# A spectral layer and a dense layer, twice: first rows straight from x, scales on the small matrix, turns row by row, W2 in pieces, the filter rebuilt

## Chip, cores and metric

One core of a Trainium2 chip. The time is device time in microseconds of one execution of the whole kernel; the runs of the kernel before took 1265.25 us (median of 3 runs, 1263.46 to 1265.83).

## What is computed

`x` is 2048 x 1024 in bf16. Two different residual layers, A and B, run one after the other, and then both once more with the same weights:

```python
def A(x, w_r, w_i):              # spectral layer
    X = rfft2(x.astype(float32)) * (w_r + 1j * w_i)
    return irfft2(X, s=(2048, 1024)).astype(bfloat16)

def B(x, w1, b1, w2):            # dense layer, F = 3584
    h = x @ w1 + b1
    sp = log1p(exp(-abs(h))) + where(h > 0, h, 0)
    return (h * tanh(sp)) @ w2   # Mish

x = x + A(layernorm(x)); x = x + B(layernorm(x))
x = x + A(layernorm(x)); x = x + B(layernorm(x))
```

The layernorm takes the mean of each row away, so column 0 of the transform is zero; the kernel uses columns 1 to 512 of the filter alone.

## The kernel before

Everything runs on one core, with x resident in SBUF as `XS` (16 tiles of 128 rows). Work is written in program order for each engine; a helper records each operation with the buffers that it reads and writes and puts semaphore waits in front of it, so that each engine's queue (PE, DVE, ACT, POOL, SP) runs strictly in the order written. All DMAs are issued through one helper line, L242.

**Layer A** splits the transform. A row index n is 128 n2 + n1, a column is 128 h + l. `XR` holds the normalised x with the 128 pairs (n2, h) on the partitions. To get there each normalised tile is written to `xn_scratch` in memory and read back in another shape (`xn_store`, `xr_load`, L460 to L470), both on POOL's queue. Stage S1 (`s1`, L486) multiplies `XR` for each n1 by the 128 x 128 matrix `M` (the transforms over n2 and over h in one) into `Y`. Then 8 groups of two k2 slots go through a pipeline of 12 steps: s2 (the rest of the transform over columns, tables FD), s3 (over n1, tables FT, and the product with the filter on DVE), i1 and i2 (back, tables BT and BD). In each step, group g is in s2, g-1 in s3, g-3 in i1 and g-4 in i2. i2 leaves `U` of its group, 128 l on the partitions and 16 components; `u_turn` (L708) writes it to `u_scratch` in memory and reads it back into `UT` with the components on the partitions, both on SP's queue. The tables of the next groups are loaded behind it on the same queue.

The filter needs reversed rows: in the first layer A `filter_bins` (L546) loads raw rows of w_r and w_i (`WR`), lets 12 matmuls for each group reverse them, copies the parts together into `WT` (POOL and ACT), and also stores `WT` in `w_scratch`. The second layer A loads `WT` from there.

**Layer B** begins with the last stage of the transform, `i4` (L759): 128 columns of `UT` against `MT`, added to `XS` by DVE (L770), rows of the first 8 tiles first. Then the statistics (DVE L412, ACT L393), `scales` (an inverse square root by iteration on DVE, L429 to L443), `apply` (L455, ACT L453), and `transposed` (L798). The first dense matmul `mm1` (L816, Mish on ACT L820) goes over 4 chunks c of 512 rows, two at a time, in 14 rounds fg; the second half of `i4` is spread over the first 8 rounds. W1 comes in 14 pieces for each pair of chunks, each reloaded as soon as the last reader of its buffer is through. W2 is loaded in round 8, in four DMAs, since its place overlaps `UT` and `Y`. `mm2` (L833, added by DVE L838) goes tile by tile; in the first layer B it also makes the statistics, scales and the normalised tile for the next layer A, stored and reloaded as above; loads of the first 12 tiles are written behind chunk 2, because `XR` overlaps the activations of that chunk.

Of the kernel before, what the change touches and what calls it, by code (L numbers as in the profile page):

```python
# [7 lines left out]
P = 128  # L8
# [111 lines left out]
def make_tables():  # L120
    n2, dh = np.arange(16.0), np.arange(8.0)
    reps = [None] * P
    for g in range(8):
# [3 lines left out]
        for kd, c in ((0, 0), (4, 1)):  # L127
            own += [(a, 3, c), (b, 3, c)] + [(s, kd, cc) for (s, cc) in low]
# [7 lines left out]
    cD = np.concatenate([8 * (np.arange(64.0) + 1), 4 + 8 * np.arange(64.0)])  # L136
# [13 lines left out]
    gain[63] = 0.5  # L150
# [14 lines left out]
    return dict(M=M.transpose(1, 0, 2).reshape(P, P), MT=M.reshape(P, P).T, JT=np.concatenate([J, -J, J0, -J0], axis=1),  # L165
# [9 lines left out]
class KB:  # L175
# [120 lines left out]
    def build(self):  # L296
# [3 lines left out]
        self.con = {k: v.ap().bitcast(BF) for k, v in con.items()}  # L300
        self.xn_d = nc.dram_tensor("xn_scratch", (16, P, self.D), BF, kind="Internal").ap()
        self.u_d = nc.dram_tensor("u_scratch", (8, P, 16, P), BF, kind="Internal").ap()
        self.w_d = nc.dram_tensor("w_scratch", (16, P, 2, 512), BF, kind="Internal").ap()
        from contextlib import ExitStack
        with ExitStack() as es:
            def sb(name, shape, dtype=BF):
                return es.enter_context(nc.sbuf_tensor(name, [P] + shape, dtype))
            self.XS = sb("XS", [16, self.D])
# [9 lines left out]
            self.RS = sb("RS", [4, 16], F32)  # L318
            self.PS = es.enter_context(nc.psum_tensor("PS", [P, 8, 512], F32))
# [40 lines left out]
    def prologue(self):  # L360
        sp, dve = self.sp, self.dve
        for j in range(16):
            self.dma(sp, self.XS[:, j, :], self.x[0, j * P:(j + 1) * P, :], f"x{j}", writes=[self.r_xs[j]])
        self.dma(sp, self.M[:], self.con["M"], "m", writes=[self.r_m])
        jt = self.alloc("JT", self.o["JT"], [4 * P])
        self.JT, self.r_jt = jt.ap, jt.res
        self.dma(sp, jt.ap, self.con["JT"], "jt", writes=[jt.res])
        self.dma(sp, self.FD[:], self.con["FD"], "fd", writes=[self.r_fd])
        self.junk = self.alloc("JUNK", self.o["JUNK"], [self.D])
        self.w1_next = 0  # L370

    def constants(self):

        sp, dve = self.sp, self.dve
        self.dma(sp, self.BD[:], self.con["BD"], "bd", writes=[self.r_bd])
# [4 lines left out]
        self.op(dve, lambda e: e.tensor_copy(self.B1[:], self.B1h[:]), reads=[r], writes=[self.r_b1])  # L380
# [7 lines left out]
    def stats_act(self, j):  # L388
        act = self.act
        x, sums, rs = self.XS[:, j, :], self.BN[:, j, 0:2], self.r_mv[j]  # L390
        rs.begin()
        for i, f in enumerate((ACT.Copy, ACT.Square)):
            self.op(act, lambda e, i=i, f=f: e.activation(self.junk.ap, x, f, accum_out=sums[:, i:i + 1]),  # L393
                    reads=[self.r_xs[j]], writes=[self.junk.res], parts=[rs])
# [65 lines left out]
    def xn_store(self, j, b):  # L460
        b.unread = False
        self.dma(self.pool, self.xn_d[j], b.ap, "xw" + b.res.name[2:], reads=[b.res], writes=[self.r_xnd[j]])

    def open_xr(self):
        self.XR = self.alloc("XR", self.o["XR"], [P, P])
        self.XR.res.begin()

    def xr_load(self, j):
        self.dma(self.pool, self.XR.ap[j:P:16, :, :], self.xn_d[j].rearrange("n (h l) -> h n l", l=P), f"xr{j % 4}",
                 reads=[self.r_xnd[j]], parts=[self.XR.res])  # L470

# [14 lines left out]
    def s1(self):  # L486
# [480 lines left out]
```

## Time and profile before

| what | us |
|---|---|
| median of 3 runs | 1265.25 |
| profiled execution, its time | 1271.47 |
| its span, first to last instruction | 1269.7 |
| PE busy with matmuls | 976.2 |
| DVE, ACT, POOL busy | 366.8, 315.1, 85.4 |

A busy PE is one that has a matmul in its pipeline. Views show the start of a group of instructions in us, how long it lasts, the engine, the line, and what was written from what; "idle before" is how long the engine stood before it and what ended that. "SPq" and "POOL ... DMA_DIRECT2D" are issues of DMAs, not transfers. Buffers in the common region of SBUF are all shown as ARENA.

### The profile page before, as it was taken

How to read it: one execution, taken by the hardware profiler on the slowest of the kernel's cores; microseconds unless marked ns; L12 is line 12 of the kernel's file. 1: busy time of each engine (PE TensorE's matmuls, PEld its weight loads, DVE VectorE, ACT ScalarE, POOL GpSimd, SP SyncE). 2: the span in 40 equal slices, each digit the busy share in tenths (PEclk: the TensorE clock that was granted, in tenths of full speed). 3: DMA queues.
4: the chain of work that ended last, by engine and by line, in shares of the span. 5: the costliest groups of instructions: out<-in, count | busy, mean ns of one | idle time of the engine just before them, and what ended most of it. 6: DMA issues, size and time to landing. Idle time of an engine off the chain costs nothing.

```text
span 1269.7 us, 13587 instructions
## 1 busy us (share of the span) xinstructions
PE 976.2 (77%) x5737; PEld 509.6 (40%) x5832; DVE 366.8 (29%) x755; ACT 315.1 (25%) x430; POOL 85.4 (7%) x132
## 2 busy tenths in 40 slices
PE   0000698449969999999997387449959999999998
PEld 0000566325424444444443354334424444444444
DVE  3220486172501443000433286282410111000111
ACT  6000466143321001432000265333312000343000
POOL 0222352000000000000031100000000000000000
PEclk9999998679979999999999598779979999999999
DMA  9333257701462001220069227731272000220000
GB/s 289 74 76 79 78 163 189 167 24 51 140 208 67 25 20 39 76 74 1 26 60 121 59 86 192 153 71 45 87 250 84 25 17 26 83 67 17 17 26 25
DMA packets 130988, 107.19 MB, mean 84 GB/s; under 512 B 43504, under 2 KB 109168, under 8 KB 130928
## 3 DMA queue, kind: packets, MB, share of 16 engines
q1 hardware_dynamic: 123760, 89.41, 25.1%
q0 software_dynamic: 7168, 16.91, 7.9%
q8 instruction: 46, 0.75, 0.3%
q14 instruction: 14, 0.11, 0.0%
HBM read 81.01 MB, written 25.17 MB: 84 GB/s over the span
## 4 chain that ended last, share of the span: by engine, by line
PE 63%; DMA 18%; DVE 9%; issue 5%; ACT 3%; POOL 3%; SPq 0%; DVEq 0%; POOLq 0%; ACTq 0%
PE PS L816 30%; PE PS L833 27%; DMA xn_scratch<-ARENA 9%; POOL ARENA L242 3%; DMA ARENA<-in_B_w_dram 2%; DVE XS L770 1%; PE PS L798 1%; DMA ARENA<-c_bt 1%; DMA u_scratch<-ARENA 1%; DVE BN L412 1%; DMA ARENA<-c_ft 1%; ACT ARENA L635 1%; PE PS L657 1%; DMA ARENA<-xn_scratch 1%; PE PS L494 1%
## 5 line engine op out<-in xcount | busy, mean ns | idle before, releaser
L816 PE MATMUL PS<-ARENA 128*128 128x512 bf16 x1750 | 394.9, 384 | 36.7 <-DMA ARENA<-in_B_w_dram 25.7
L833 PE MATMUL PS<-ARENA 128*128 128x512 bf16 x1754 | 387.7, 379 | 2.0
L816 PEld LDWEIGHTS PS<-ARENA 128*128 128x128 bf16 x1792 | 175.5, 99 | 247.6 <-issue 38.4
L820 ACT ACTIVATE ARENA<-PS,B 128x512 bf16<-128x512 f32 x224 | 153.4, 687 | 471.7 <-PE PS L816 471.6
L833 PEld LDWEIGHTS PS<-ARENA 128*128 128x128 bf16 x1792 | 174.7, 98 | 207.6
L838 DVE TENSOR_TENSOR XS<-PS,XS 128x512 bf16<-128x512 f32 x64 | 44.2, 691 | 562.3 <-PE PS L833 562.3
L494 PE MATMUL PS<-M,ARENA 128*128 128x128 bf16 x256 | 20.9, 257 | 166.5 <-DMA ARENA<-xn_scratch 166.3
L494 PEld LDWEIGHTS PS<-M,ARENA 128*128 128x128 bf16 x256 | 19.7, 119 | 167.9 <-issue 166.7
L500 ACT ACTIVATE ARENA<-PS 128x1024 bf16<-128x1024 f32 x16 | 16.1, 1022 | 244.1 <-PE PS L494 243.7
L412 DVE BATCH_NORM_STATS2 BN<-XS 128x6 f32<-128x512 bf16 x104 | 67.1, 674 | 4.8 <-DMA XS<-in_A_x_dram 3.6
L770 DVE TENSOR_TENSOR XS<-PS,XS 128x512 bf16<-128x512 f32 (+1 forms) x48 | 38.9, 861 | 100.3 <-PE PS L765 100.3
L455 DVE TENSOR_SCALAR ARENA<-XS,RS 128x1024 bf16<-128x1024 bf16 x56 | 29.4, 544 | 78.7 <-DMA xn_scratch<-ARENA 77.9
L657 PE MATMUL PS<-ARENA 128*128 128x256 bf16 x256 | 39.4, 306 | 14.2 <-DMA ARENA<-c_bt 14.2
L242 POOL DMA_DIRECT2D xn_scratch<-ARENA x32 | 18.4, 576 | 450.2 <-DVE ARENA L455 450.2
L242 POOL DMA_DIRECT2D ARENA<-xn_scratch x32 | 34.2, 1072 | 139.4 <-DMA xn_scratch<-ARENA 119.8
L765 PE MATMUL PS<-MT,ARENA 128*128 128x64 bf16 x512 | 21.8, 206 | 27.5 <-issue 26.5
L635 ACT ACTIVATE ARENA<-PS 128x1024 bf16<-128x1024 f32 x32 | 32.9, 1027 | 33.6 <-PE PS L631 33.6
L798 PE MATMUL PS<-IDENT,ARENA 128*128 128x128 bf16 x256 | 21.8, 240 | 23.1 <-DVE ARENA L455 22.0
L664 ACT ACTIVATE ARENA<-PS 128x1024 bf16<-128x1024 f32 x32 | 32.8, 1025 | 24.6 <-PE PS L657 24.6
L657 PEld LDWEIGHTS PS<-ARENA 128*128 128x128 bf16 x256 | 27.4, 109 | 26.9 <-issue 15.9
L393 ACT ACTIVATE ARENA<-XS 128x1024 bf16<-128x1024 bf16 x24 | 25.3, 1056 | 49.9 <-DVE XS L770 44.8
L502 DVE CAST ARENA<-PS 128x1024 bf16<-128x1024 f32 x16 | 18.8, 1218 | 59.3 <-PE PS L494 59.2
(52 smaller groups left out, 524.4 us busy)
## 6 DMA issues: line engine op xcount, KB each, us to landing
ARENA<-in_B_w_dram SPq DMA_DIRECT2D x56, 512.0 KB, 3.8
ARENA<-in_B_w_dram SPq DMA_DIRECT2D x8, 1792.0 KB, 16.0
xn_scratch<-ARENA POOLq DMA_DIRECT2D x32, 256.0 KB, 5.4
ARENA<-xn_scratch POOLq DMA_DIRECT2D x32, 256.0 KB, 6.4
u_scratch<-ARENA SPq DMA_DIRECT2D x16, 512.0 KB, 3.3
ARENA<-u_scratch SPq DMA_DIRECT2D x16, 512.0 KB, 5.2
XS<-in_A_x_dram SPq DMA_DIRECT2D x16, 256.0 KB, 6.1
w_scratch<-ARENA SPq DMA_DIRECT2D x16, 256.0 KB, 3.3
```

Of the source, the lines that this page charges most:

```text
L242: return eng.dma_start(out_ap, in_ap).then_inc(ds.sem, 16)
L412: self.op(self.dve, lambda e: e.bn_stats(self.BN[:, j, 6 * h:6 * h + 6], self.XS[:, j, 512 * h:512 * h + 512]), reads=[self.r_xs[j]], part ...
L494: fns.append(lambda e, q=q, j=j, ps=ps: e.matmul(ps[:, q * P:(q + 1) * P], self.XR.ap[:, 8 * j + q, :], M[:], start=True, stop=True))
L635: self.op(act, lambda e: e.activation(x.ap.rearrange("p a b -> p (a b)"), ps, ACT.Copy, scale=SIG), reads=banks, writes=[x.res])
L657: fns.append(lambda e, c=c, part=part: e.matmul(ps[:, c * 256:(c + 1) * 256], yk.ap[:, part, c * P:(c + 1) * P], t[:, (128, 0)[part]:(384, ...
L664: self.op(act, lambda e: e.activation(v.ap[:, :, i, :], src, ACT.Copy), reads=banks, parts=[v.res])
L770: self.op(self.dve, lambda e: e.tensor_tensor(xs, src, xs, ALU.add), reads=rb, parts=self.r_xs[lo:lo + 8])
L798: fns.append(lambda e, db=db: e.transpose(PSb[:, bank, db * P:(db + 1) * P], xn.ap[:, db * P:(db + 1) * P], self.IDENT[:]))
L816: fns.append(lambda e, db=db, bank=bank, fl=fl: e.matmul(PS[:, bank, :], wb.ap[:, db, fl * P:(fl + 1) * P], x.ap[:, db, :], start=(db == 0 ...
L820: self.op(act, lambda e, bank=bank, ft=ft: e.activation(at.ap[:, ft, :], PS[:, bank, :], ACT.Mish, bias=self.B1[:, ft:ft + 1]), reads=[sel ...
L833: fns.append(lambda e, ft=ft: e.matmul(PS[:, bank, :], at.ap[:, ft, t * P:(t + 1) * P], W2[ft // 7].ap[:, ft % 7, h * 512:(h + 1) * 512], ...
L838: self.op(dve, lambda e: e.tensor_tensor(xs, PS[:, bank, :], xs, ALU.add), reads=[self.r_bank[bank]], writes=[self.r_xs[j]])
```

## The change

- First layer A: `XR` is loaded straight from x in 32 DMAs on SP, and x itself in 4 DMAs. The scale of each row goes on the matrix instead: `first_scales` computes all 16 tiles' scales, turns them with a spread and one fp32 transpose so that each partition (n2, h) has its scale for each n1, and makes 128 scaled copies of the matrix (`MN`) on DVE and ACT. The means are not taken away; they fall on column 0 alone.
- `u_turn` writes each component (row of `UT`) directly from `U` by a DMA of its own, 8 after each half of i2, from SP, POOL and, for the last group, ACT.
- Tables and filter rows are loaded from POOL's queue, `xn_store` moves to SP's. The filter is rebuilt in the second layer A too; `w_scratch` and `u_scratch` go. Copies in `filter_bins` are merged by two.
- `i4` does the first 4 tiles, then the next 4 through ACT into a buffer that DVE adds later; the second half starts in round 2, four at a time.
- W2 comes in 28 pieces, two in each round, and mm2 sums in that order.
- The last tile of the first layer B goes to `XR` by 8 DMAs from SBUF, without memory. Some table layouts, buffer places and the engine of a few copies change.

```diff
     def prologue(self):
+        for c in range(4):
+            self.dma(sp, self.XS[:, 4 * c:4 * c + 4, :], xt[:, 4 * c:4 * c + 4, :], f"x{c}", writes=self.r_xs[4 * c:4 * c + 4])
...
+        xv = self.x[0].rearrange("(n2 n1) (h l) -> h n2 n1 l", n2=16, l=P)
+        for q in range(4):
+            r = Res(f"xr{q}")
+            for h in range(8):
+                self.dma(sp, self.XR.ap[h:P:8, 32 * q:32 * q + 32, :], xv[h][:, 32 * q:32 * q + 32, :], f"xr{q}", parts=[r])
+            self.r_xr.append(r)
+        self.dma(sp, self.FD[:], self.con["FD"], "fd", writes=[self.r_fd])
-        for j in range(16):
-            self.dma(sp, self.XS[:, j, :], self.x[0, j * P:(j + 1) * P, :], f"x{j}", writes=[self.r_xs[j]])
     def constants(self):
-        self.op(dve, lambda e: e.tensor_copy(self.B1[:], self.B1h[:]), reads=[r], writes=[self.r_b1])
+        self.op(self.pool, lambda e: e.tensor_copy(self.B1[:], self.B1h[:]), reads=[r], writes=[self.r_b1])
     def xn_store(self, j, b):
-        self.dma(self.pool, self.xn_d[j], b.ap, "xw" + b.res.name[2:], reads=[b.res], writes=[self.r_xnd[j]])
+        self.dma(self.sp, self.xn_d[j], b.ap, "xw" + b.res.name[2:], reads=[b.res], writes=[self.r_xnd[j]])
+    def xr_direct(self, j, b):
+        for h in range(8):
+            prog = self.act if h % 2 else self.sp
+            self.dma(prog, self.XR.ap[16 * h + j:16 * h + j + 1, :, :], b.ap[:, h * P:(h + 1) * P], "xd" + prog.name,
+                     reads=[b.res], parts=[self.XR.res])
+    def first_scales(self):
+        for j in range(0, 16, 4):
+            for i in range(2):
+                self.stats_dve(j + i)
+                self.stats_act(j + 2 + i)
+            self.sums_to_mv(j + 2, 2)
+        self.scales(0, 16)
...
+        for j in range(16):
+            for q in range(8):
+                n = 8 * j + q
+                if q % 3 == 2:
+                    self.op(act, lambda e, n=n: e.activation(self.MN.ap[:, n, :], self.M0.ap, ACT.Copy, scale=rc[:, n:n + 1]),
+                            reads=[rt.res, self.M0.res], parts=[self.r_mn[j]])
+                else:
+                    self.op(dve, lambda e, n=n: e.tensor_scalar(self.MN.ap[:, n, :], self.M0.ap, rc[:, n:n + 1], None, op0=ALU.mult),
+                            reads=[rt.res, self.M0.res], parts=[self.r_mn[j]])
     def s1(self, li):
-            self.group(fns, reads=[self.XR.res, self.r_m], writes=banks)
+                m = M[:] if li else self.MN.ap[:, n, :]
...
+            self.group(fns, reads=[self.r_xr[j // 4], self.r_m if li else self.r_mn[j]], writes=banks)
     def layer_A(self, li):
         def load_tabs(g):
-            self.dma(sp, FT[g % 3].ap, self.con["FT"][g], f"ft{g % 3}", writes=[FT[g % 3].res])
+            self.dma(pool, FT[g % 3].ap, self.con["FT"][g], f"ft{g % 3}", writes=[FT[g % 3].res])
         def load_w(g):
+            for c, src in enumerate((self.w_r, self.w_i)):
+                rows = src.rearrange("(k s) d -> k s d", s=16)[:, a:b + 1:b - a, 1:513]
+                self.dma(pool, wr.ap[:, c, :, :], rows, f"wr{g % 4}", parts=[wr.res])
         def filter_bins(g):
-                self.dma(sp, self.w_d[s], wt.ap, f"ws{n}", reads=[wt.res], writes=[self.r_wd[s]])
-        def u_turn(g):
-            self.dma(sp, self.u_d[g], u.ap, f"uw{g % 3}", reads=[u.res], writes=[self.r_ud[g]])
-            self.dma(sp, self.UT.ap[g:P:8, :, :], self.u_d[g].rearrange("l r n -> r l n"), f"ur{g % 3}",
-                     reads=[self.r_ud[g]], parts=[self.UT.res])
+        def u_turn(g, half):
+            for i in range(8):
+                r = 8 * half + i
+                prog = sp
+                if g == 7 and i % 2:
+                    prog = act
+                elif g < 7 and i % 4 == 3:
+                    prog = pool
+                self.dma(prog, self.UT.ap[r * 8 + g:r * 8 + g + 1, :, :], u.ap[:, r, :], f"u{prog.name}{g % 3}",
+                         reads=[u.res], parts=[self.UT.res])
-                if 0 <= g2 < 8 and h == 0 and li == 0:
+                if 0 <= g2 < 8 and h == 0:
                     filter_bins(g2)
     def layer_B(self, li, last):
-        for u in range(8):
-            self.i4(16, 0, (2 * (u % 4), 2 * (u % 4) + 1), 16 * u)
+        for u in range(4):
+            self.i4(0, 4, 32 * u, 32, 2 * u)
         for c in range(2):
+            if c:
+                for j in range(4, 8):
+                    self.op(dve, lambda e, j=j: e.tensor_tensor(self.XS[:, j, :], self.XS[:, j, :], YS.ap[:, j - 4, :], ALU.add),
+                            reads=[YS.res], writes=[self.r_xs[j]])
...
+            if c == 0:
+                for u in range(4):
+                    self.i4(4, 4, 32 * u, 32, 2 * (u % 3), staged=YS)
-                xn[4 * c + t] = self.apply(act if t % 2 else dve, 4 * c + t)
+                xn[4 * c + t] = self.apply(dve, 4 * c + t)
...
-            while nb < min(16, 2 * (fg + 1)):
-            if fg == 8:
-                W2 = load_w2()
+                while nb < min(16, 4 * (fg - 1)):
+            for _ in range(2):
+                if w2_order and (w2_order[0] >= 16 or nb == 16):
+                    load_w2(w2_order.pop(0))
```

## Rows read from the trace of the kernel before

**Rows 1.** The page: busy tenths of PE in 40 slices.

```profile
PE   0000698449969999999997387449959999999998
```

**Rows 2.** The list of waits: waiter <- waited for: us in total, times, longest.

```profile
PE PS L494 <- DMA ARENA<-xn_scratch: 166.3, 2, 136.2
...
PE PS L765 <- issue: 26.5, 2, 13.3
...
PE PS L816 <- DMA ARENA<-in_B_w_dram: 25.7, 2, 13.6
...
PE PS L657 <- DMA ARENA<-c_bt: 14.2, 5, 5.4
```

**Rows 3.** Busy time by stretch; the last two numbers are DMA share and GB/s.

```profile
4.00:8.00 4.00, 0.00 (x0) 0.00 (x0) 2.42 (x6) 1.90 (x3) 0.00 (x0) 1.00 1.02 334
...
136.20:147.80 11.60, 10.30 (x128) 9.65 (x128) 9.42 (x8) 8.00 (x8) 1.04 (x3) 1.00 0.01 2
...
247.00:249.00 2.00, 0.00 (x0) 0.00 (x0) 0.00 (x0) 0.00 (x0) 0.00 (x0) 0.50 1.35 170
...
650.00:655.00 5.00, 4.95 (x24) 2.29 (x24) 1.85 (x5) 0.00 (x0) 2.89 (x3) 1.00 1.08 74
```

**Rows 4.** Timeline of the front: start, us, engine, line, what.

```profile
9.27 0.54 SPq L242 DMA_DIRECT2D M<-c_m  x1
...
9.85 0.43 SPq L242 DMA_DIRECT2D ARENA<-c_jt  x1
...
13.03 0.16 DVE L443 SCALAR_TENSOR_TENSOR RS<-MV,RS 128x4 f32<-128x4 f32 x1
...
13.23 1.92 DVE L455 TENSOR_SCALAR ARENA<-XS,RS 128x1024 bf16<-128x1024 bf16 x4
...
25.16 0.19 ACT L393 ACTIVATION_READ_ACCUMULATOR ARENA<-XS 128x1 f32 x1
...
33.49 0.59 POOL L242 DMA_DIRECT2D xn_scratch<-ARENA  x1
```

**Rows 5.** Groups of instructions by shape: busy us, mean ns of one, idle before.

```profile
L455 DVE TENSOR_SCALAR ARENA<-XS,RS 128x1024 bf16<-128x1024 bf16 x56 | 29.4, 544 | 78.7 <-DMA xn_scratch<-ARENA 77.9
...
L639 DVE TENSOR_TENSOR ARENA<-ARENA 128x1024 bf16<-128x1024 bf16 x32 | 22.4, 699 | 31.0 <-ACT ARENA L635 31.0
...
L567 POOL COPY ARENA<-ARENA 128x192 bf16<-128x192 bf16 x32 | 21.2, 690 | 38.9 <-DVE ARENA L641 38.9
...
L575 ACT ACTIVATE ARENA<-PS 128x192 bf16<-128x192 f32 x32 | 8.2, 334 | 6.4 <-DVE ARENA L641 3.4 <-PE PS L557 1.9 <-DVE ARENA L644 0.7
...
L429 DVE TENSOR_SCALAR RS<-MV 128x1 f32<-128x1 f32 x16 | 2.5, 153 | 0.6
```

**Rows 6.** Timeline of both layers A and the beginnings of both layers B.

```profile
181.62 0.32 SPq L242 DMA_DIRECT2D u_scratch<-ARENA  x1
...
209.03 0.32 SPq L242 DMA_DIRECT2D u_scratch<-ARENA  x1
...
237.01 1.02 ACT L706 ACTIVATE ARENA<-PS 128x1024 bf16<-128x1024 f32 x1 [1.14 <-PE PS L696]
...
244.84 0.54 SPq L242 DMA_DIRECT2D ARENA<-u_scratch  x1
...
250.30 1.92 PE L765 MATMUL PS<-MT,ARENA 128*128 128x64 bf16 x33 [13.32 <-issue]
...
365.35 1.87 PE L816 MATMUL PS<-ARENA 128*128 128x512 bf16 x4 [12.11 <-DMA ARENA<-in_B_w_dram]
...
731.17 2.02 PE L590 MATMUL PS<-FD,ARENA 128*128 128x256 bf16 x19 [1.21 <-DVE ARENA L502]
...
827.48 2.72 PE L765 MATMUL PS<-MT,ARENA 128*128 128x64 bf16 x48 [13.14 <-issue]
```

**Rows 7.** Timeline from the first layer B to the second layer A.

```profile
688.98 0.55 DVE L455 TENSOR_SCALAR ARENA<-XS,RS 128x1024 bf16<-128x1024 bf16 x1 [8.66 <-DMA xn_scratch<-ARENA]
...
719.21 1.01 PE L494 MATMUL PS<-M,ARENA 128*128 128x128 bf16 x8 [30.05 <-DMA ARENA<-xn_scratch]
```

More of the change, by code (lines that the diff above doesn't have):

```diff
@@ L126, in make_tables @@
         own = [(s, kd, c) for kd in (1, 2) for c in (0, 1) for s in (a, b)]
-        for kd, c in ((0, 0), (4, 1)):
+        for kd, c in ((4, 0), (0, 1)):
             own += [(a, 3, c), (b, 3, c)] + [(s, kd, cc) for (s, cc) in low]
@@ L502, in s1 @@
                 self.op(self.dve, lambda e, dst=dst, src=src: e.tensor_copy(dst, src), reads=banks, parts=[self.Y.res])
+        for r in ([self.MN.res, self.M0.res] + self.r_xr if not li else []):
+            r.r(self.pe, self.pe.count)
+            self.XR.res.r(self.pe, self.pe.count)
     def layer_A(self, li):
         if li == 0:
-            self.xn_ring()
-            self.open_xr()
-            for j in range(0, 16, 4):
-                for i in range(2):
-                    self.stats_dve(j + i)
-                    self.stats_act(j + 2 + i)
-                self.sums_to_mv(j + 2, 2)
-                self.scales(j, 4)
-                for i in range(4):
-                    self.xn_store(j + i, self.apply(self.dve, j + i))
-                    self.xr_load(j + i)
+            self.junk = self.alloc("JUNK", self.o["U"], [self.D])
+            self.first_scales()
         K = 1024
@@ L579, in zslot @@
+                self.op(act, lambda e, d3=d3, src=src: e.activation(d3[:, :, :, 64:128], src, ACT.Copy),
+                        reads=banks, parts=[wt.res])
         def zslot(g, i):
@@ L831, in mm2 @@
             fns = []
-            for ft in range(NF):
-                fns.append(lambda e, ft=ft: e.matmul(
-                    PS[:, bank, :], at.ap[:, ft, t * P:(t + 1) * P], W2[ft // 7].ap[:, ft % 7, h * 512:(h + 1) * 512],
-                    start=(ft == 0), stop=(ft == NF - 1)))
+            order = list(range(16, 28)) + list(range(16))
+            for i, ft in enumerate(order):
+                fns.append(lambda e, i=i, ft=ft: e.matmul(
+                    PS[:, bank, :], at.ap[:, ft, t * P:(t + 1) * P], W2[ft].ap[:, h * 512:(h + 1) * 512],
+                    start=(i == 0), stop=(i == NF - 1)))
             self.group(fns, reads=ra + r_w2, writes=[self.r_bank[bank]])
@@ L887, in layer_B @@
             self.r_xs[j].begin()
-        nb = 0
+        nb, w2_order = 0, list(range(16, 28)) + list(range(16))
         for fg in range(14 + 2):
@@ L893, in layer_B @@
                 for t in range(4):
[L894 removed]
+                    transposed(1, t, xn[4 + t], act if t % 2 else dve)
             if fg >= 2:
                 mm1(1, fg - 2)
[L897 to L901 removed]
+                while nb < min(16, 4 * (fg - 1)):
+                    self.i4(8, 8, 8 * nb, 8, 3 + nb % 3)
+                    nb += 1
+            for _ in range(2):
+                if w2_order and (w2_order[0] >= 16 or nb == 16):
+                    load_w2(w2_order.pop(0))
+        assert not w2_order
         r_w2 = [b.res for b in W2]
@@ L926, in layer_B @@
             mm2(3, t, 1)
-            if not last:
+            if not last and t < 3:
                 self.xr_load(12 + t)
```

186 lines of the change are left out of this document (100 added, 86 removed).

## The prediction

> **What bounds the kernel now.** I read the busy shares first: PE is busy for three quarters of the span, and its slices [rows 1] (31.7 us each) show runs of nines, which are the dense layers, and holes: four empty slices at the start, thinner stretches after them and again around slices 22 to 27, and a notch in the middle of each run of nines. The dense matmuls are untouched by the change, so all that can be won lies in the holes. The list of waits [rows 2] then says what ends them: PE's first matmul waits for the XR load (two waits, 136.2 and 30.1 us, one for each spectral layer), the dense layer waits twice for weights, i1 waits for its tables, and i4 stands twice for 13.3 us under "issue". That last one is no issue time: the UT load of the last group left at 244.84 and i4 starts at 250.30 [rows 6], 12.3 us after ACT finished U at 238.0, which is a store to memory, a load behind it and two landings. The timeline of the front [rows 4] shows why it is long: the 16 tiles go store, land, load, store, each behind the other on POOL's queue, while ACT had its last statistic at 25.4 us. So 110 us of the front are the round trip through memory and nothing else.
>
> The sum is made against the profiled execution, 1271.5 us (span 1269.7 and 1.8 around it); it lies 6.2 over the median of 1265.25, and I subtract 6 at the end.
>
> **Front of layer 0.** Removed: 16 stores and 16 loads on POOL, and the 16 applies that waited for them. Added: XR straight from x (32 DMAs of 128 KB on SP, 256-byte pieces into 16 partitions), scales put on 128 copies of the 16x8 matrix. Two chains run side by side, and the later one counts.
> Chain of scales: the statistics are the same instructions. x now comes in four 1 MB pieces, so DVE starts some 2.5 us later, but ACT, which sets the end, had to wait for the third tile before too, which is most of the first piece; I keep its end at 25.4 [rows 4]. Then 3 + 9 small DVE steps at 0.2 us (start to start, 13.03 to 13.23 [rows 4]) make 27.8. The spread of the scales, the fp32 transpose and the copy back are three handovers of about 0.4 us: 28.9. Then 96 copies of the matrix on DVE and 32 on ACT. No row has this form on DVE. Bounds: a tensor_scalar of one column lasts 0.153 us and four large ones start 0.46 apart at 0.544 each, an overlap of 0.08, so 0.07 us at least; the large one, cut from 1024 to 128 columns at the slope of these two rows, is 0.20, so 0.20 at most [rows 4, 5]. I take 0.16, near the upper end since these read a scale from memory as the large one does: 15.4 us, so 44.3. ACT's 32 are 0.28 us by its 192-column copy of 0.334 [rows 5], perhaps 0.38 with a scale that is read: 12 us, covered by DVE's. S1 behind it takes 11.6 us [rows 3] less some 1.6 that PE runs ahead in four PSUM pairs: 54.3.
> Chain of data: x, 4.19 MB, at 334 GB/s [rows 3] ends near 14.5 us. XR is 4.19 MB too, in 256-byte pieces. The row nearest is the UT load, 170 GB/s (16 partitions, SP's queue, same pieces): 24.7 us. The other end is the XR load on POOL's queue, 74 GB/s into 8 partitions: 57 us. I take the first, since form and queue are the same. The filter rows and tables, 2.9 MB from POOL, share the DMA engines: 8.6 us. With 2 us of landing the last quarter is there at 50, and its four S1 tiles (2.9 us) end at 53.
> So S1 ends at about 56 instead of 147.8: **92 us** (88 with slower copies, 100 at best, 71 with XR at 74 GB/s). B1's cast now stands in POOL's queue before the filter copies, behind a load that lands at about 56, and the copies are due at 64; that costs nothing with 8 us of room.
>
> **Layer A, from S1 to i4.** Before: 102.5 us in layer 0 and 96.3 in layer 1 (731.17 to 827.48 [rows 6]). The groups' steps are 9.1 us (first U store at 181.62, fourth at 209.03 [rows 6]), filled by PE, so up to there I change nothing in layer 0. Four groups are left then; PE waits there for tables, because SP's queue holds them behind the UT load, which waits for the store: 14.2 us for BT alone over both layers [rows 2]. With tables on POOL about 3 us remain (5 us landing against steps of 4), and the last U is ready at about 229 instead of 238.
> Now each group's turn is 16 DMAs of one UT row (32 KB into one partition), 12 on SP. An SP issue of such a 32 KB load took 0.54 us, others 0.43 [rows 4]: 12 are 5.9 us a group. That is hidden under a step of 9.1 but not under the last four, which PE does in 5.5, 4, 4 and 3 us. So SP's issue sets the end: fourth group through at 212, three groups at 5.9, then 8 rows on SP beside 8 on ACT, 4 us, and one landing of 2.4 (the load took 5.5 from issue to i4, of which 512 KB at 170 GB/s are 3.1 [rows 3, 6]): 236.1. i4 starts there instead of 250.3: **14 us**. ACT's eight issues stand before its last U copy, which shifts it by up to 2 us; this is inside the 4 us.
> Layer 1 gets the filter rebuilt, 12 matmuls and the copies in each of 8 steps, where before it loaded it ready. I therefore give it layer 0's length, 88.5 us from S1's end to i4, against 96.3: **8 us**, between 4 lost and 12. POOL's load: copies worth four of 192 columns at 0.69 and four of 128, two thirds of that, 4.6 us a step [rows 5], and up to six DMA issues at 0.6 [rows 4]: 8 of 9.1 us. It fits with little room.
>
> **i4 and the second layernorm.** The first half goes in two: four groups of 32 narrow matmuls, PE at 47 ns each by [rows 6] (33 in 1.92 us including start-up): 1.5 us a group, so four tiles are ready after 7.2 us instead of 10.2. The other four tiles come through ACT and cost DVE four more adds of 0.70 [rows 5], 2.8 us, while two ACT applies of 1.2 go. ACT is free sooner for its first Mish. Between 0 and 6 us in each layer; **3 each**, 6 in all.
>
> **W2 in pieces.** The two stalls are 25.7 us [rows 2]; after each, PE runs at half its pace for a while (4 matmuls in 1.87 us at 365.35 [rows 6], 0.43 us apart instead of 0.215), some 2 us more. The pieces bring 0.5 MB beside 0.5 MB of W1 in each round of 6.9 us, that is 150 GB/s against the 334 shown, and the last pieces are out two rounds ahead of mm2: **30 us** (25 to 32).
>
> **From layer B to layer A.** PE is empty from 689.2 to 719.2 [rows 7]. Stores leave POOL's queue, so the loads start at 641 rather than 645.4 and DVE's apply doesn't wait (8.7 us at 688.98 [rows 7]). The last tile: two DVE steps of 0.7, some 11 small ones, the apply 0.55: 3.9 us after PE's end; eight row DMAs on SP and ACT 2 us, landing 2.4 to 4. The 15 loads at 74 GB/s (256 KB, 3.55 us each) end at 694.3 + 2. S1 can start at about 699: **20 us** (16 to 23).
>
> Sum: 92 + 14 + 8 + 6 + 30 + 20 = 170. 1271.5 - 170 = 1101.5, on the median's scale **1096 us**.
>
> **Rivals.**
> 1. *Rows written at half SP's issue rate.* The turn's rows take 0.75 to 1.0 us instead of 0.5, 9 to 12 us a group. Then the turn runs behind from the first group (its first half is ready at 177.6): i4 at 177.6 + 8 x 9 + 2.4 = 252, or 276: 16 to 40 us later in each layer, 1127 to 1175, middle 1140. For it: 16 engines write into one partition. Against it: row DMAs of different partitions overlap.
> 2. *The partition is the limit, slower than before.* The loads reach 74 GB/s into 8 partitions and 170 into 16 [rows 3]: about 10 GB/s for each partition, twice. If that is a limit of the destination, one row takes 3.1 us; 12 behind one another on SP are 37 us a group, i4 starts at 476, 240 later in each layer: 1576. It decides for slower from 1.5 us a row on SP (8 x 17.7 us a group eats the 170). Against it: the 8-partition load ran on another queue, and packets spread over fewer engines would show the same pair of rates. The Trainium skill (SBUF - State Buffer, section Door 1: The DMA port swizzle) speaks against the change in the same sense: a transfer's rate goes with the ports that its partitions reach, and four partitions on one port measured 27.6 GB/s. As an estimate by that page a row would be 1.2 us, 12 of them 14.3, and the time 1096 + 2 x 58 = 1211; the trace agrees in direction, and no row here has a single destination partition.
> 3. *XR binds the front* at 74 GB/s: S1 ends at 77: 1117.
> 4. *The W2 stall only moves*, since pieces and W1 share SP's queue, or mm2 waits for its last pieces: up to 30 back, 1126. The rate above speaks against it.
>
> **How the numbers follow.** Forecast 0.56, rival 1 0.22, rival 2 0.09, rival 3 0.10, rival 4 0.03. The forecast's own range is 1074 (front 100 instead of 92, layernorms 6 each, A and the boundary 8 better) to 1115 (the low ends of A, W2 and the boundary). The range runs to the end of rival 1: 1074 to 1178, and leaves rival 2 out. About 0.2% is what a measurement of this kernel can tell from no change; 0.01 lies there, on the way from rival 1 to 2. Faster 0.91, slower 0.08.
>
> **What would show it.** The first S1 matmul near 30 us and S1's end near 56, with the wait in front of it on DVE (scales) and not on the XR load; i4 some 88 us after S1's end in both layers, with SP issuing row DMAs back to back in the last four groups; no wait of the dense layer for weights; S1 of layer 1 about 10 us after the dense layer's last matmul. Wrong it would be if the row DMAs take over 0.75 us each in a queue, or if filter copies on POOL hold up the products.

## The result, and the profile after

| | before | after |
|---|---|---|
| median of 4 runs | 1265.54 us (1263.46 to 1269.44) | 1150.57 us (1143.32 to 1150.91) |
| ratio after / before, of the means | | 0.9075 (0.9033 to 0.9117) |
| profiled execution, its span | 1271.5, 1269.7 us | 1150.72, 1148.9 us |

The kernel became 9.3% faster: 120.8 us between the two spans, where 170 were forecast. The time lies inside the stated range of 1074 to 1178 and 55 us over the predicted 1096; 6 of the 55 are the step from the profiled execution to the median that the prediction subtracted, since after's profiled execution lies at its median. Cut at the same instructions of the two timelines (first and last matmul of S1, first of s2, of i4 and of mm1, last of mm2), the spans differ so:

| stage, us | before | after | gained | forecast |
|---|---|---|---|---|
| front: start to the first s2 | 147.85 | 60.48 | 87.4 | 92 |
| layer A(0): first s2 to first i4 | 102.5 | 109.3 | -6.9 | 14 |
| first i4 to first mm1, both layers | 45.1 | 35.6 | 9.5 | 6 |
| first mm1 to the end of mm2, both layers | 832.7 | 802.8 | 30.0 | 30 |
| end of mm2 to S1 of layer 1 | 30.05 | 15.7 | 14.4 | 20 |
| S1 of layer 1 | 12.0 | 11.5 | 0.5 | 0 |
| layer A(1): first s2 to first i4 | 96.3 | 110.4 | -14.1 | 8 |

So nearly all that is missing is in layer A, 43 of 49 us: it did not get shorter, it got longer in both layers. The page's PE slices of after (28.7 us each; [rows 1] of before):

```profile
PE   0388636999999999999958884489999999999998
```

One empty slice at the start is left of four, and the notch in the dense layers is gone. The list of waits (waiter <- waited for: us in total, times, longest) now reads, in answer to [rows 2]:

```profile
PE PS L813 <- DMA ARENA<-ARENA: 37.5, 2, 20.3
PE PS L524 <- DVE ARENA L521: 33.0, 1, 33.0
PE PS L552 <- DMA ARENA<-ARENA: 15.7, 1, 15.7
PE PS L700 <- DMA ARENA<-c_bt: 15.0, 4, 4.5
PE PS L552 <- DVE ARENA L560: 11.8, 1, 11.8
```

In the front PE waits for DVE: for the scales before their transpose (L524), then, a quarter into S1, for copies of Y (L560), which stand in DVE's queue behind the scaled copies of the matrix. The 25.7 us on weights have no successor. But the rows (ARENA<-ARENA) hold i4 (L813) for 37.5 us where it stood 26.5 before, they hold S1 of layer 1 (L552), and the tables of i1 (L700) come as late as before (14.2), though they left SP's queue. The page's list of DMA issues (KB of each, median us from issue to landing) shows how slowly both land:

```profile
ARENA<-ARENA SPq DMA_DIRECT2D x188, 32.0 KB, 6.6
...
ARENA<-c_bt POOLq DMA_DIRECT2D x16, 192.0 KB, 6.7
```

The end of layer A(0) in the chain of waits (start, us, what) is SP's last row, its landing, i4; the same at the turn to layer 1:

```profile
160.39 0.60 SPq L242
161.03 0.60 SPq L242
161.68 0.60 SPq L242
162.32 7.38 DMA ARENA<-ARENA
169.71 0.09 issue
169.79 1.03 PE PS L813 x32
```

```profile
595.04 9.35 DMA ARENA<-ARENA
604.39 0.35 issue
604.74 1.33 PE PS L552 x11
```

And one steady step of the groups, from the timeline (start, us, engine, line): POOL's filter copies lie on the product that the next step waits for.

```profile
108.02 0.54 POOL L242 DMA_DIRECT2D ARENA<-c_bt  x1
...
108.56 0.88 POOL L613 COPY ARENA<-ARENA 128x384 bf16<-128x384 bf16 x1
...
109.42 1.96 DVE L682 TENSOR_TENSOR ARENA<-ARENA 128x1024 bf16<-128x1024 bf16 x1 [2.45 <-ACT ARENA L678]
...
109.97 0.86 POOL L613 COPY ARENA<-ARENA 128x384 bf16<-128x384 bf16 x1
...
111.31 1.12 DVE L684 TENSOR_TENSOR ARENA<-ARENA 128x1024 bf16<-128x1024 bf16 x1
```

The first product took 0.699 us in the mean before [rows 5]. DVE's U copies (L747) stand 10.3, 10.5 and 10.5 us apart here, 9.2, 9.2 and 8.8 before.

The last tables of layer 0, from the timelines of POOL and PE: the last BT load stands directly behind two rows in POOL's own queue, and i1 waits for the last two of these loads.

```profile
132.98 1.07 POOL L242 DMA_DIRECT2D ARENA<-ARENA  x2 [0.20 <-issue]
134.04 0.54 POOL L242 DMA_DIRECT2D ARENA<-c_bt  x1
```

```profile
136.05 1.86 PE L700 MATMUL PS<-ARENA 128*128 128x256 bf16 x8 [4.47 <-DMA ARENA<-c_bt]
...
145.05 1.46 PE L700 MATMUL PS<-ARENA 128*128 128x256 bf16 x8 [3.96 <-DMA ARENA<-c_bt]
```

### The profile page after: what moved, and what is told of

Its sections match the earlier page's. It is cut to its first block, busy times and chain, and to the rows that moved or that the text cites. A ratio compares the mean times of both kernels' runs of the same rounds, so it can differ in the third digit from the quotient of the medians.

```text
span 1148.9 us, 14586 instructions
## 1 busy us (share of the span) xinstructions
PE 981.6 (85%) x6091; PEld 522.5 (45%) x6185; DVE 383.5 (33%) x813; ACT 332.9 (29%) x466; POOL 139.6 (12%) x204
## 4 chain that ended last, share of the span: by engine, by line
PE 72%; DVE 13%; DMA 5%; SPq 4%; ACT 3%; issue 2%; ACTq 0%; POOL 0%; DVEq 0%
PE PS L886 33%; PE PS L868 32%; SPq L242 4%; DMA ARENA<-ARENA 2%; DMA XS<-in_A_x_dram 2%; DVE ARENA L682 2%; PE PS L605 1%; DVE ARENA L539 1%; PE PS L633 1%; DVE BN L427 1%; DVE XS L819 1%; PE PS L850 1%; DVE ARENA L689 1%; DVE ARENA L560 1%; DVE ARENA L684 1%
## 5 line engine op out<-in xcount | busy, mean ns | idle before, releaser
L868 PE MATMUL PS<-ARENA 128*128 128x512 bf16 x1752 | 385.3, 379 | 5.5 <-DVE ARENA L855 2.0
L886 PE MATMUL PS<-ARENA 128*128 128x512 bf16 x1754 | 387.4, 379 | 2.0
L242 POOL DMA_DIRECT2D ARENA<-xn_scratch x15 | 15.9, 1068 | 417.1 <-PE PS L886 388.3
L813 PE MATMUL PS<-MT,ARENA 128*128 128x32 bf16 (+1 forms) x768 | 24.6, 188 | 45.7 <-DMA ARENA<-ARENA 37.5
L819 DVE TENSOR_TENSOR XS<-PS,XS 128x512 bf16<-128x512 f32 (+1 forms) x40 | 29.1, 789 | 87.8 <-PE PS L813 87.8
L700 PE MATMUL PS<-ARENA 128*128 128x256 bf16 x256 | 37.5, 295 | 15.0 <-DMA ARENA<-c_bt 15.0
L813 PEld LDWEIGHTS PS<-MT,ARENA 128*128 128x128 bf16 x768 | 23.0, 101 | 49.1 <-issue 41.6
L408 ACT ACTIVATE ARENA<-XS 128x1024 bf16<-128x1024 bf16 x24 | 25.4, 1056 | 56.2 <-DVE XS L819 40.8
L700 PEld LDWEIGHTS PS<-ARENA 128*128 128x128 bf16 x256 | 26.6, 105 | 25.4 <-issue 15.8
L242 POOL DMA_DIRECT2D ARENA<-ARENA x56 | 30.2, 543 | 65.1 <-DVE ARENA L747 52.4
L682 DVE TENSOR_TENSOR ARENA<-ARENA 128x1024 bf16<-128x1024 bf16 x32 | 30.2, 943 | 23.1 <-ACT ARENA L678 23.0
L721 PE MATMUL PS<-ARENA,BD 128*128 128x256 bf16 x192 | 28.8, 293 | 9.5 <-DVE ARENA L747 9.2
L633 PE MATMUL PS<-FD,ARENA 128*128 128x256 bf16 (+1 forms) x312 | 34.0, 258 | 2.8 <-DVE ARENA L560 2.4
L613 POOL COPY ARENA<-ARENA 128x384 bf16<-128x384 bf16 x32 | 29.4, 920 | 10.4 <-DVE ARENA L684 10.4
```

The costliest lines, as they stand in the source:

```text
L242: return eng.dma_start(out_ap, in_ap).then_inc(ds.sem, 16)
L633: fns.append(lambda e: e.matmul(dst, at(r), FD[:, t:t + dst.shape[-1] * 2], start=start, stop=stop))
L682: self.op(dve, lambda e: e.tensor_tensor(ta.ap, x.ap, wt.ap[:, 0:1, :].to_broadcast([P, 2, 512]), ALU.mult), reads=[x.res, wt.res], writes ...
L700: fns.append(lambda e, c=c, part=part: e.matmul(ps[:, c * 256:(c + 1) * 256], yk.ap[:, part, c * P:(c + 1) * P], t[:, (128, 0)[part]:(384, ...
L813: fns.append(lambda e, l=l: e.matmul(ps[:, w * l:w * l + w], self.UT.ap[:, u0 + l, :], self.MT[:, 8 * lo:8 * lo + w], start=True, stop=True))
L819: self.op(self.dve, lambda e: e.tensor_tensor(xs, src, xs, ALU.add), reads=rb, parts=self.r_xs[lo:lo + nb])
```

## The experiments

Lengths are those of the table's layer A rows, layer 0 / layer 1; after has 109.3 / 110.4.

**rows_spread.** The same row DMAs, but each written over all partitions.

```diff
-self.dma(prog, self.UT.ap[r * 8 + g:r * 8 + g + 1, :, :], u.ap[:, r, :], ...
+self.dma(prog, self.UT.ap[:, r * 8 + g, :], u.ap[:, r, :], ...
```

> The kernel after, with one change: every row DMA of the turn writes its 32 KB over all 128 partitions (a slice of UT of 256 bytes in each) instead of into one partition. Number, size, queues and waits of the DMAs are the same; what lands in UT is not the turned matrix, so this leaves the transposition out. In the kernel after, from S1's end to i4 takes 109.3 us in layer 0 and 110.4 in layer 1, SP issues the last rows one every 0.64 us, and i4 starts 7.4 us after SP's last row. Theory 'issue': SP's 0.64 us is what it costs to issue a row, whatever its destination; then it stays between 0.60 and 0.66, only the landing gets shorter (to some 2.5 us), and i4 comes 5 us sooner in each layer: total 1141. Theory 'partition': the write into one partition holds the queue back; then SP's row falls to the 0.43 to 0.54 us that its other 32 KB loads took, the last 39 rows end 4 to 8 us sooner, landing 2.5: 9 to 13 us in each layer, total 1125 to 1133.

Measured 1137.5 us (1136.4 to 1139.7), lengths 102.4 / 103.9. Its DMA issues and the end of its chain:

```profile
ARENA<-ARENA SPq DMA_DIRECT2D x188, 32.0 KB, 1.9
...
ARENA<-c_bt POOLq DMA_DIRECT2D x16, 192.0 KB, 2.9
```

```profile
158.85 0.60 SPq L242
159.49 0.60 SPq L242
160.14 1.86 DMA ARENA<-ARENA
162.00 0.09 issue
162.09 1.03 PE PS L813 x32
```

Both theories hold a part. SP's issue stays at 0.60 to 0.64 us, so that is the issue's own price and not the partition's. The landing falls from 6.6 to 1.9 us, and the tables land in 2.9 instead of 6.7, though they are issued as late as in after. The list of waits shows what that is worth:

```profile
PE PS L700 <- DMA ARENA<-c_bt: 3.2, 2, 1.7
```

So rows that go into one partition delay the tables. Whether SP's rows do it, or the two rows that stand ahead of each table in POOL's own queue, is open: in after the last of these lands at 144.45 and the table behind it at 144.91, and no run took POOL's rows away alone. With the tables on time the last U is ready 10 us sooner (146.4 instead of 156.6), yet i4 is only 7.7 sooner, because now SP's backlog of rows alone sets it. The steps stay at 10.3 to 10.6, so they have another cause.

**turn_memory.** The turn alone undone: one store and one load a group on SP; everything else of the change stays.

```diff
-for i in range(8): ... self.dma(prog, self.UT.ap[r * 8 + g:r * 8 + g + 1, :, :], u.ap[:, r, :], ...
+if half:
+    self.dma(sp, self.u_d[g], u.ap, ...)
+    self.dma(sp, self.UT.ap[g:P:8, :, :], self.u_d[g].rearrange("l r n -> r l n"), ...)
```

> The kernel after, with the turn of U undone alone: one store of 512 KB and one load of 512 KB for each group on SP's queue, as in the kernel before; the tables and filter rows stay on POOL's queue. Theory 'the turn by rows pays nothing': the turn through memory takes 12.3 us from the last U to i4 (kernel before), the rows 13.2 (156.6 to 169.8), and POOL is rid of two to four DMA issues that wait for U in each step; the steps go from 10.5 us back to 9.3 and the tables come sooner, so S1's end to i4 falls from 109 to 96 to 102: total 1128 to 1138. Theory 'the rows pay, and the loss is elsewhere' (the rebuilt filter alone lengthens the steps): the steps stay at 10.5, i4 comes within 3 us of where it is, total 1147 to 1157.

Measured 1118.7 us (1118.3 to 1119.6), lengths 94.2 / 94.3: 32 us faster than after, more than either theory gave. The steps are 9.5, 9.5 and 8.8, PE no longer waits for tables in the last groups (DVE's U copies 3.3, 3.7 and 3.0 us apart, where after has 9.1, 9.0 and 3.5), the last U ends at 138.5, and i4 follows 15.3 later (13.2 in after). Of layer 0's 15.1 us the steps are 3.6 and the last groups 11.6. ACT's last U copy gives 2.8 more, since it no longer stands behind ACT's row issues; 2.1 go back behind the last U, and 0.8 ahead of the first. Of the 11.6, 8.4 are PE's two waits for BT; most of the rest is PE's lower clock behind them: in after, the eight i1 matmuls after each wait take 1.86 and 1.46 us instead of 1.04, and the granted clock, after PE had stood idle, is 0.79 from 132 to 140 us, a mean of the levels 1.2 and 2.4 GHz; in turn_memory it is 1.00 from 120 to 139. What is left is SP's queue, from its timeline: store, load and store stand behind one another.

```profile
138.36 0.54 SPq L242 DMA_DIRECT2D ARENA<-u_scratch  x1
139.00 1.16 SPq L242 DMA_DIRECT2D u_scratch<-ARENA  x1
143.80 0.54 SPq L242 DMA_DIRECT2D ARENA<-u_scratch  x1
144.44 1.25 SPq L242 DMA_DIRECT2D u_scratch<-ARENA  x1
149.31 0.54 SPq L242 DMA_DIRECT2D ARENA<-u_scratch  x1
```

**pool_order.** POOL's rows, tables and filter rows of a step issued behind the next step's filter copies.

```diff
-load_tabs(g3 + 2)
+later.append(lambda g=g3 + 2: load_tabs(g))   # rows on POOL, load_w, load_btabs likewise
 ...
 filter_bins(g2)
+for fn in later: fn()
```

> The kernel after, with one change in POOL's queue: the rows, tables and filter rows of a step stand behind the filter copies of the next step instead of ahead of them (in the steps without filter copies they go out at the step's end). Nothing is left out. Theory 'order': a step takes 10.5 us instead of 9.1 because POOL waits for U, issues rows and tables and only then copies the filter, and these copies then lie on DVE's first product (1.96 us instead of 0.69); with the copies first, that product goes back to 0.7 and the step to 9.2 us, over some six steps of each layer 7 to 9 us: total 1133 to 1138, if the rows at the end (25 to 39 on SP at 0.64) start sooner by as much. Rival 'amount': POOL and DVE share what they share however the copies lie, another product gets longer instead: total within 3 us of 1150.6.

Measured 1163.7 us (1161.6 to 1164.9), lengths 115.7 / 117.8: neither. The theory of the order fell. The first product is back at 0.69 us, but the last one of the step, which stands ahead of the U copy, now meets the copies (timeline of DVE and POOL):

```profile
112.56 1.95 DVE L689 TENSOR_TENSOR ARENA<-ARENA 128x512 bf16<-128x512 bf16 x1
```

```profile
112.76 0.88 POOL L613 COPY ARENA<-ARENA 128x384 bf16<-128x384 bf16 x1
113.56 0.65 POOL L616 COPY ARENA<-ARENA 128x256 bf16<-128x256 bf16 x1
```

Two of the three steps are 10.3 us instead of 10.3 and 10.5, as the rival said; the third is 8.8. The 13 us are lost elsewhere: the first U comes 2.4 and 3.1 us later after the first s2, the last groups take 1.0 and 5.8 us more, and in layer 0 i4 follows the last U 4.7 us later. Tables leave and land later (7.3 us for BT; PE waits 4.5 us at FT, where after has no such wait), but PE's waits for BT are 15.0 us as in after, so how much of the 13 is theirs isn't shown.

**filter_ready.** In layer 1 the filter is loaded, not rebuilt.

```diff
-if 0 <= g2 < 8 and h == 0:
+if 0 <= g2 < 8 and h == 0 and li == 0:
     filter_bins(g2)
+# li == 1: self.dma(pool, wt.ap, <2 KB a partition from memory>, ...) for each slot
```

> The kernel after, with the filter of layer 1 not rebuilt: its tiles are loaded, two DMAs of 256 KB a group on POOL's queue, from other data of the right shape, so the layer 1 product is not the reference's (left out: the 12 matmuls, 4 POOL copies and 2 ACT copies of each of 8 steps). Layer 0 must stay at 109.3 us. Theory 'copies': in layer 1 the steps go from 10.5 to 9 us, S1's end to i4 from 110.4 to 99 to 102: total 1139 to 1142. Rival 'rows': SP's 0.64 us a row sets the end whatever the steps do (128 rows less those of POOL and ACT, 100 x 0.64 = 64 us, all but the first groups being behind one another): layer 1 stays within 3 us, total 1148 to 1151.

Measured 1135.2 us (1133.7 to 1138.0), lengths 110.1 / 100.2. Beside rows the rebuilt filter costs layer 1 10 us, as the theory of the copies said. But the steps, where it saw this, give 4.4 (the first three take 27.0 instead of 31.4); the larger part, 8.0, lies ahead of the first U (23.4 us after the first s2 instead of 31.4), and 2 are lost again at the end. 2.4 us more come at the turn between the layers (13.3 instead of 15.7), where fewer bytes are under way. In turn_memory the filter is rebuilt too, the first U comes at 32.5, and layer 1 is still 2 us shorter than in the kernel before (94.3 against 96.3). What a ready filter would give there was not run.

**w2_block.** W2 back in four DMAs in the ninth round.

```diff
-for _ in range(2):
-    if w2_order and (w2_order[0] >= 16 or nb == 16): load_w2(w2_order.pop(0))
+if fg == 8: load_w2()   # 4 x [7, D]
```

> The kernel after (1150.6 us) with W2 loaded as in the kernel before: four DMAs of 1.8 MB, all at the ninth round of the dense layer, and summed in the order 0 to 27. It sizes the W2 term, which the prediction put at 30 us for both layers. From the first matmul of mm1 to the last of mm2 the kernel before took 416.4 us in layer 0, the kernel after 401.4. Theory 'pieces are worth the whole': it goes back to 416, two stalls of 13 us on weights come back, total 1176 to 1182. Rival 'part of it is the layernorm's and i4's': 5 to 10 us a layer, total 1161 to 1170.

Measured 1176.9 us (1176.1 to 1177.7): 26.3 us slower, mm1 to the end of mm2 415.2 and 415.1 us instead of 401.4, and in the list of waits the stall is back:

```profile
PE PS L868 <- DMA ARENA<-in_B_w_dram: 22.8, 2, 11.7
```

**late_filter.** turn_memory, with layer 1's filter rows and tables of groups 1 to 3 held back until XR is whole.

```diff
+late = lambda g: [self.XR.res] if li and 0 < g < 4 else []
-self.dma(pool, wr.ap[:, c, :, :], rows, ...)
+self.dma(pool, wr.ap[:, c, :, :], rows, ..., reads=late(g))   # FT, BT likewise
```

> The kernel turn_memory (1118.7 us), where in layer 1 the filter rows and tables of groups 1 to 3 (1.9 MB on POOL's queue) are loaded only after XR is complete. In the kernel after the last tile's eight rows of XR need 9.35 us from their issue at 595.0 to landing while POOL's queue moves filter rows at over 100 GB/s beside them. Theory 'crowding': without these loads the rows land in 2 to 4 us, S1 of layer 1 starts 5 to 7 us sooner (9 to 11 us after the dense layer instead of 15.9), total 1112 to 1114, unless the second group's filter then comes late (up to 3 us back). Rival 'one partition is slow by itself': the landing stays at 8 to 9 us, total within 2 us of 1118.7 or later by the late filter.

Measured 1114.3 us (1113.9 to 1115.0). The last of the eight rows lands in 4.4 us instead of 9.35, from its chain:

```profile
579.59 4.42 DMA ARENA<-ARENA
584.00 0.31 issue
584.31 6.02 PE PS L554 x56
```

S1 starts 10.7 us after the dense layer, where the forecast had 10: the missing 5 us of the boundary were crowding by the change's own loads.

**store_act.** turn_memory, with U's stores on ACT's queue.

```diff
-self.dma(sp, self.u_d[g], u.ap, ...
+self.dma(act, self.u_d[g], u.ap, ...
```

> The kernel turn_memory (U turned through memory, 1118.7 us), with the stores of U issued on ACT's queue instead of SP's; the loads stay on SP. In turn_memory the chain between 132.7 and 153.8 us is store, load issue, store, load issue, store, load: each store stands in SP's queue behind the load of the group before, which waits for the store before that (5.6, 4.8 and 4.9 us), and i4 starts 15.3 us after the last U. Theory 'queue': with the stores on another queue only the last store and load remain, 0.5 + 3.2 + 0.5 + 4.4 = 8.6 us behind the last U, i4 6 to 7 us sooner in each layer, total 1104 to 1107. Rival 'throughput': the window 125 to 150 us moves 173 to 184 GB/s, the last three groups are 3 MB of stores and loads, 17 us from 132 on, so i4 comes at 150 and the gain is 3 to 4 a layer: total 1111 to 1113.

Measured 1111.7 us (1109.4 to 1112.7), lengths 89.9 / 88.6: the rival's time. The chain is short now, but the load of the last group takes 7.6 us where one alone took 4.4:

```profile
138.62 3.31 DMA u_scratch<-ARENA
141.95 7.56 DMA ARENA<-u_scratch
149.51 0.09 issue
149.60 1.03 PE PS L810 x32
```

**combined.** store_act and late_filter together, and the load of group 6 on ACT's queue.

```diff
+for q, prog in ([(6, act), (7, sp)] if g == 7 else [(g, sp)] if g < 6 else []):
-self.dma(sp, self.UT.ap[g:P:8, :, :], self.u_d[g]...
+    self.dma(prog, self.UT.ap[q:P:8, :, :], self.u_d[q]...
```

> store_act (1111.7 us) with late_filter's change and one more: the UT load of group 6 goes on ACT's queue, behind the store of group 7, so that the last two loads stand in two queues. Late filter rows are worth 4.5 us (1118.7 to 1114.3). In store_act the last load took 7.6 us from the store's landing to i4 in layer 0, two loads of 512 KB one behind the other. Theory 'queue': side by side they take 4.4, i4 comes 3 us sooner in each layer, total 1101. Rival 'DMA engines': both share what there is, total 1106 to 1108.

Measured 1107.6 us (1106.9 to 1109.1): late_filter's gain and nothing for the second queue (lengths 90.6 / 90.9, last load 6.7 us). From 140 us until the last load is in, the DMA engines show a busy share over 1 and nearly the same rate in both runs (224 GB/s in store_act, 218 here), so a second queue finds nothing free, as the rival said.

**rows_last.** store_act with group 7 alone turned by rows, eight on SP and eight on ACT.

```diff
+if g == 7: ... prog = act if i % 2 else sp
+    self.dma(prog, self.UT.ap[r * 8 + g:r * 8 + g + 1, :, :], u.ap[:, r, :], ...
```

> The kernel store_act with one difference: the last group alone (g = 7) is turned by rows, eight on SP and eight on ACT, as in the kernel after; groups 0 to 6 go through memory. It asks whether a few rows with nothing else in their queues are quick. After the last U copy four rows on SP are 2.6 us. Theory 'rows are slow to land in any case' (6.6 us at the median in the kernel after, 9.4 at the turn between the layers where only eight were under way): 0.5 + 2.6 + 6.6 to 9.4 = 10 to 12.5 us from the last U to i4, and ACT's last U copy 2 us later: 4 to 6 us a layer slower than store_act. Theory 'only the crowd of rows is slow': landing 2 to 3 us, 5.5 to 6 us from the last U to i4, even with store_act or 1 us a layer better.

Measured 1121.4 us (1120.0 to 1123.2), lengths 97.1 / 94.8, 6 to 7 us a layer slower than store_act. The chain ends:

```profile
150.12 0.60 SPq L242
150.77 6.32 DMA ARENA<-ARENA
157.08 0.05 issue
157.13 1.05 PE PS L816 x32
```

The rows were not alone: the loads of groups 5 and 6 move beside them until 151.6. ACT's first two rows, issued before these loads, land in 2.8 us each; from the fourth on it is 6 to 10.5. So a row into one partition is not slow in any case, and how sixteen would land by themselves isn't shown. ACT's last U copy also came later behind its row issues, by 2.8 us in layer 1 (81.7 after the first s2, 78.9 in store_act); in layer 0 2.2 us of the loss stand ahead of the first U, before any row. Turning the last group by rows lost here, i4 following the last U by 13.0 and 13.1 us where store_act has 11.1 and 9.7.

**x_tiles.** turn_memory with x in 16 pieces.

```diff
-for c in range(4): self.dma(sp, self.XS[:, 4 * c:4 * c + 4, :], ...
+for j in range(16): self.dma(sp, self.XS[:, j, :], ...
```

> The kernel turn_memory (1118.7 us) with x loaded in 16 pieces of 256 KB, as in the kernel before, instead of four of 1 MB. In the kernel after ACT's last statistic ends at 30.2 us instead of 25.2 and S1 ends at 60.5 (forecast 56). Theory 'pieces': ACT and DVE had to wait for whole pieces of four tiles; with 16 the statistics end at 25 to 26, S1's first matmul comes at 30 instead of 35, its end 4 to 5 us sooner: total 1114. Rival 'XR next': twelve more issues on SP at 0.5 us push the 32 loads of XR 6 us back, the last issue goes from 42 to 48 and S1 ends within 1 us of where it was: total 1118 to 1120.

Measured 1122.4 us (1121.1 to 1123.8), S1's first matmul at 35.7 instead of 35.1: the pieces are not the cause. (The total is 3.7 us over turn_memory, above the rival's 1118 to 1120 too; this was not followed up.) A piece issued at 8.1 us lands 13.1 later, beside XR and the filter rows:

```profile
8.09 13.13 DMA XS<-in_A_x_dram
```

**x_first.** combined, with XR and POOL's loads of layer 0 started only when x has landed.

```diff
-late = lambda g: [self.XR.res] if li and 0 < g < 4 else []
+late = lambda g: ([self.XR.res] if li else self.r_xs[12:]) if li == 0 or 0 < g < 4 else []
 # and XR's first load with reads=self.r_xs[12:]
```

> combined, and in layer 0 the loads of XR and POOL's loads of filter rows and tables start only when x has landed. x in 16 pieces alone (x_tiles) brought nothing: its last pieces still landed at 21.2 us. Theory 'crowding': x lands at 14.5 to 16 when nothing moves beside it (20.7 in the kernel after), ACT's last statistic is at 25 to 26 instead of 30, S1's first matmul at 30 to 31 instead of 35, S1's end at 55.5 to 57 instead of 60: 4 us less than combined. Rival 'XR then binds': SP issued XR's 32 loads from 8 to 42 us; if they need these 34 us in any case, the last quarter is there at 50 to 52, S1 ends at 55 to 58 (2 to 4 us less), and if more, nothing is won.

Measured 1101.9 us (1099.9 to 1103.7), ratio to before 0.8683 (0.8667 to 0.8699), the fastest of all. The last piece of x lands at 14.1 us (23.2 in after). ACT's last statistic starts at 25.0 us, S1 at 33.1, the first s2 at 55.1 (60.1 in combined), from its timeline:

```profile
25.03 0.19 ACT L410 ACTIVATION_READ_ACCUMULATOR ARENA<-XS 128x1 f32 x1
```

```profile
33.09 1.14 PE L554 MATMUL PS<-ARENA 128*128 128x128 bf16 x9 [4.62 <-DVE ARENA L541]
...
55.14 1.05 PE L637 MATMUL PS<-FD,ARENA 128*128 128x256 bf16 x8 [1.19 <-DVE ARENA L562]
```

S1's start now waits for XR, whose first quarter lands at 33.0, held back behind x; S1's end is still set by the copies on DVE, which free its PSUM. XR and POOL's loads were held back together, so which of them had crowded x isn't separated.

## Why the prediction was right, and where it was not

**The range.** That 1150.6 lies inside it is owed to the range's upper end, which was rival 1's: the forecast's own range ended at 1115. The way of the change and its two largest terms were right; the term for layer A had the wrong sign.

**What bounds it: right.** The gain lies in the holes named in [rows 1, 2]; the wait in front of S1's first matmul is on DVE's scales, as forecast.

**Front, 92 forecast, 87.4 measured.** The copies were sized right (96 in 15.7 us, forecast 15.4). S1's end at 56 stood 1.7 over the longer of its own two chains, 54.3, without a reason; that covered part of the miss. The step that failed is "I keep its end at 25.4": the 334 GB/s of [rows 3] were x moving alone, and the change sets the filter rows, then XR, beside it, and x landed at 23.2. ACT's last statistic came at 30.2. x_first takes the crowd away: 25.2, and the front gains 92.7.

**W2, 30 forecast, 30.0 measured,** and 26 to 28 when undone. **i4 and layernorm, 6 forecast, 9.5 measured,** near the upper end of the 0 to 6 us a layer. Which of their parts gave more was not tried.

**Boundary, 20 forecast, 14.4 measured.** The failed step is the landing, "2.4 to 4": 9.35 us, because the change's own filter rows and tables moved at that moment. Without them 4.4, and S1 comes at 10.7 instead of 15.7.

**Layer A, +22 forecast, -21 measured: wrong, in four steps.**
1. "12 are 5.9 us a group": the 0.49 us came from loads out of memory [rows 4]; a row out of the arena costs SP 0.64, 7.7 us a group, wherever it goes (rows_spread). Where SP's backlog sets the end, in rows_spread, layer A is still 102 to 104 us, with steps of 10.5.
2. "One landing of 2.4": taken from a load into 16 partitions. Into one partition, among many such rows, it is 6.6 at the median and 7.4 at the end; ACT's eight issues also held its last U copy up by 2.8, not the 2 allowed for.
3. "With tables on POOL about 3 us remain": 15.0 remained in both layers, as the rows delay the tables' landing (6.7 us; in rows_spread it is 2.9, and 3.2 remain). This was the largest piece: the last groups are 11.6 of the 15.1 us that undoing the turn gives back in layer 0.
4. "Up to there I change nothing": the steps went from 9.1 to 10.5. POOL waits for U, issues rows and tables and copies late, onto DVE's products. That filter copies on POOL might hold up products stood in the prediction as a sign of error, and so it came. With the turn undone the steps are 9.5, and without the copies (layer 1 of filter_ready) 9.0 in the mean, so it takes both, the rows and the copies.

Of the 14 us of layer A(0), 9 were the tables' (last U at 229 instead of 238) and 5 the turn's (i4 7 us behind the last U instead of 12.3). The first part held once the turn was undone: in turn_memory the last U comes 11.2 us sooner after the first s2 than in the kernel before, PE's waits for BT, 14.2 us over both layers [rows 2], are gone from its list, and A(0) gains 8.2; the turn by rows costs 15. For layer 1 "layer 0's length" was right to 2.4 us in every run but filter_ready (94.3 against 94.2 in turn_memory).

**The rivals.** Rival 1 gave 1127 to 1175, the nearest to 1150.6 (the middle of these two is 1151, not the 1140 that stands beside them). Its time came for other reasons than its own: SP does issue back to back in the last groups, but at 0.64 us, under the 0.75 that I set as its sign, and the rest of the delay is tables, steps and landing. Rival 2 had the place right and the price wrong: a row doesn't occupy SP for 3.1 us, since rows of different partitions overlap: SP issues one every 0.64 us, 51 GB/s, while each takes 6.6 to land. The Trainium skill (SBUF — State Buffer, section Door 1: The DMA port swizzle) ties a transfer's rate to the ports that its partitions reach; rows_spread agrees in direction, 6.6 against 1.9 us to landing, while the 1.2 us a row estimated from it was not seen at the issuing engine. Rivals 3 and 4 did not occur. The total came as near as 55 us only because the two terms with the most weight, front and W2, were right to 5 us; layer A alone missed by 43.

## What to carry to other kernels

A transfer's cost is not only its own wait. Against the turn through memory beside it (turn_memory), the turn by rows removed 2.1 us behind layer 0's last U and cost 11.6 in the last groups, mostly at tables that came late; x and the last rows of XR were slowed by loads beside them. Undo each part of a change by itself, since a good sum can hide a part with the wrong sign; this one is 32 us faster without its row turn. When copies meet another engine's work, moving them may only choose the victim, as in pool_order.

## What the runs showed of the hardware that I had not expected

- A DMA of 32 KB from one tile of the arena to another costs SP 0.60 to 0.64 us, whether it writes one partition or 128; in the same run the loads of M, MT and IDENT, 32 KB each out of memory, took 0.43. That the source makes the difference isn't shown: XR's loads out of memory, 128 KB in pieces of 256 bytes, stood 0.67 us apart.
- The same row lands in 1.9 us over 128 partitions and in 6.6 in one, at the median, when many are under way. Rows into one partition land in 2.8 us when two are under way (rows_last) and in 3.4 to 5.1 when there are eight (late_filter), so it takes both, the one partition and the crowd. A 192 KB table behind such rows takes 6.7 instead of 2.9.
- Two queues moved two loads of 512 KB no faster than one (6.7 and 7.6 us for the last).
- A DVE product with two inputs takes 1.96 us instead of 0.69 beside POOL's copies, and a smaller one 1.95 instead of 0.42 (pool_order). The Trainium skill (SBUF — State Buffer, section SBUF: two separate sides) has the two engines share a port pair under an exclusive lock; the trace agrees in that POOL's copies ran back to back meanwhile, 0.88 and 0.65 us each.
